# Two PSUM banks for transposes and one for weight products and first-chunk products, in place of one and two, in a windowed attention with two gated MLPs

## The chip, the cores and the metric

The kernel runs on one NeuronCore of a Trainium2 chip. The metric is the device time of one launch in microseconds (us); lower is better. The median of three runs before the change is 284.13 us (283.84 to 284.21). About 0.2% is what a measurement of this kernel can tell from no change.

## The reference

Attention over 2 batches, 8 heads, 768 positions and 64 values per head: each query sees the first 8 keys and the last 96. Its output feeds a gated MLP (a causal convolution of 5 taps makes the gate, one 512x512 product the value, a second the output), and that feeds another (512 to 1024, ReLU, a convolution of 3 taps as gate, 1024 to 512). Cut to what matters:

```python
scores = scale * np.matmul(q, k.transpose(0, 1, 3, 2)) + bias    # bias: -slope * distance
scores = np.where(keep, scores, -1000000000.0)                   # first n_global keys, last n_local keys
a = softmax(scores);  x = np.matmul(a, v)                        # x: (2, 768, 512)

gate = sigmoid(causal_conv5(x))                                  # first MLP
x = gate * (x @ w_val) @ w_out

h = np.maximum(x @ w_in, 0.0)                                    # second MLP
out = (h * sigmoid(conv3(h))) @ w_out2
```

## The kernel before

**Stages.** The attention goes through 12 tiles of 128 queries, 6 for each batch. For a tile, `scores` (L493, TensorE, marked `s` by the bank it writes) makes the scores of 4 heads at a time over its own and the tile of keys before it. `least` (L504, VectorE) adds the bias and takes the row minimum, `grow` (L509, ScalarE) the exponential and its sum, L530, L533 or L536 (VectorE, GpSimd or ScalarE) divide. `turn` (L563, TensorE, bank `t`) transposes the probabilities of two heads, 4 blocks of 128x128, into one bank; L567 (ScalarE) or L573 (VectorE) copies them out to `pts`; `output` (L588, bank `x`) multiplies by the values; L605 or L611 copies the result into `x`.

**Weights.** `product` (L337, bank `f`) multiplies the first MLP's output weight with the second's input weight, so that the two become one matrix W of 512x1024. It makes 8 products of 4 matmuls each; of each, `split_ops` writes a high part `Wh` (L244, ScalarE) and a low part `Wl` (L246, VectorE), and only the low part's end hands the bank on. `parts_unit` does the same for `w_val` (`wvh`, `wvl`), with no product.

**The MLPs.** The positions are cut into 4 chunks (2 for each batch, 400 and 368 columns). `values` multiplies a chunk by `w_val`: 4 products of 12 matmuls (L253 to L255, three for each block, of high and low parts), each taken out of its bank by the gate on VectorE (L759). `hidden` multiplies by W: 8 products of 12 matmuls, each taken out by a ReLU on ScalarE (L800). `project` writes the output in the four banks of the scores.

**Banks.** All 8 PSUM banks are in use: `BANKS` (L46) says 4 for `s`, 1 for `t`, 1 for `x` and 2 for `f`. `c.bank` gives the 12 products of the first chunk the ring `f`; later chunks, which start when the attention ends, take `f`, `t`, `f`, `x` in turn. A ring hands out its buffers one after the other, and a buffer's first instruction waits for the last user of the tenant before.

**Order.** A planner (`Plan`) sets the order of every engine's instructions. It knows an estimated cost for each step, the wait for a bank or buffer among its predecessors (`link`), and lays the steps in several passes by the length of what follows them (`lay`). Steps with several ways (dividing, the copies out of `t` and `x`, the masks, a convolution's first tap) go to the engine that ends them first. At run time each engine goes through its own list strictly in order.

Of the kernel before, what the change touches and what calls it, by code (L numbers as in the profile page):

```python
# [42 lines left out]
LANDED = {("k", 1): 3.0, ("k", 2): 5.0, ("r", 1): 6.3, ("v", 1): 7.7, ("r", 2): 9.0}  # L43
LANDING = 2.4
ORDERED = {getattr(mybir.EngineType, e) for e in ("PE", "DVE", "Activation", "Pool")}
BANKS = {"s": 4, "t": 1, "x": 1, "f": 2}  # L46


def slope(h):
# [819 lines left out]
def attention_gated_mlps(ctx, tc, kq, v, nn, w_val, conv_w, w_out, w_in2, w_out2, out):  # L869
# [50 lines left out]
    def arm(fast):  # L920
        with ExitStack() as es:
            psum = es.enter_context(tc.tile_pool(name="ps", bufs=1, space=PSUM))
            pools = es.enter_context(ExitStack())
            c.psum = Ctx()
            c.psum.tile = lambda shape, dt, tag, name: psum.tile(shape, dt, tag=tag, name=name, bufs=BANKS[tag])
            pl = c.plan = Plan()
# [15 lines left out]
            def bank(tag):  # L942
                return lambda: psum.tile([P, 512], F32, tag=tag, name=tag, bufs=BANKS[tag])

            def sb(pool, tag, shape, dt, n):
                return pl.ring(n, lambda: pool().tile(shape, dt, tag=tag, name=tag, bufs=n))

            c.ring = {t: pl.ring(n, bank(t)) for t, n in BANKS.items()}
            here = lambda: sg
# [97 lines left out]
```

## Time and profile before

| what | before |
|---|---|
| median of 3 runs | 284.13 us (283.84 to 284.21) |
| the profiled execution's own time | 283.84 us |
| its span, first to last instruction | 281.9 us |
| TensorE busy | 269.6 us (96%) |
| VectorE busy | 232.2 us (82%) |
| ScalarE busy | 194.8 us (69%) |
| GpSimd busy | 90.0 us (32%) |
| granted TensorE clock | 0.999 |

In the profile PE is TensorE, DVE VectorE, ACT ScalarE and POOL GpSimd. A matmul's duration includes its way through the array, and matmuls overlap, so a busy PE says little of how many it does; what one costs in a row of them is read from the starts of two neighbours in the timeline. One matmul of 32-bit floats in L337, L493 and L588 leaves two rows, so their counts in the trace are twice those in the program. A TensorE row that waited has the time and what ended it in brackets.

### The profile page before, as it was taken

What the parts mean: (1) busy time and instruction counts of PE and PEld (TensorE: products, weight loads), DVE (VectorE), ACT (ScalarE), POOL (GpSimd) and SP (SyncE); (2) the same over time, 40 slices, a digit from 0 to 9 for tenths busy, and PEclk for the clock granted to TensorE, in tenths of its full rate; (3) what the DMA queues carried; (4) which work ended last, traced back from release to release, by engine and by line L of the source; (5) the groups of instructions that cost most, each with busy time, mean ns of one, the idle gap of its engine ahead of it and who ended that gap; (6) DMA issues with size and microseconds to landing.
All of it is one profiled execution on the core that took longest, in us unless ns stands there. A gap on an engine that the chain in (4) does not pass through costs nothing.

```text
span 281.9 us, 5430 instructions
## 1 busy us (share of the span) xinstructions
PE 269.6 (96%) x1832; PEld 226.3 (80%) x1832; DVE 232.2 (82%) x587; ACT 194.8 (69%) x496; POOL 90.0 (32%) x199
## 2 busy tenths in 40 slices
PE   2889999999999999999999999999999999999993
PEld 2767675655458989999999999889999988899883
DVE  3989999999999999999999999999984654357600
ACT  2999989998678999886797456883473254544520
POOL 4635746346353336533256001140411000002000
PEclk9999999999999999999999999999999999999999
DMA  5983877446733431003300000100000020000121
GB/s 165 356 346 97 277 243 237 141 140 216 227 87 140 144 127 49 9 2 116 121 0 0 3 0 0 40 37 1 37 2 0 0 77 37 37 1 2 38 112 49
DMA packets 10420, 26.17 MB, mean 93 GB/s; under 512 B 1424, under 2 KB 2704, under 8 KB 10384
## 3 DMA queue, kind: packets, MB, share of 16 engines
q1 hardware_dynamic: 9968, 25.22, 26.4%
q10 hardware_dynamic: 416, 0.52, 0.5%
q8 instruction: 16, 0.26, 0.4%
q14 instruction: 20, 0.16, 0.2%
HBM read 22.59 MB, written 3.15 MB: 91 GB/s over the span
## 4 chain that ended last, share of the span: by engine, by line
PE 72%; DVE 21%; issue 3%; ACT 1%; DVEq 1%; POOL 0%
PE s L254 8%; PE s L255 8%; PE s L253 8%; PE f L253 7%; PE f L254 7%; PE f L255 7%; DVE p L504 5%; PE t L563 4%; PE x L588 4%; PE s L493 4%; DVE z L706 3%; DVE raw L279 3%; PE t L255 2%; PE x L255 2%; PE x L253 2%
## 5 line engine op out<-in xcount | busy, mean ns | idle before, releaser
L706 DVE SCALAR_TENSOR_TENSOR z<-h,cw,z 128x384 f32<-128x384 f32 x64 | 40.7, 642 | 12.8 <-ACT z L701 11.6
L509 ACT ACTIVATE p<-p,st 128x256 f32<-128x256 f32 (+1 forms) x96 | 46.0, 482 | 3.8 <-DVE st L504 2.9
L708 ACT ACTIVATE z<-z 128x384 f32<-128x384 f32 (+2 forms) x48 | 24.8, 523 | 26.3 <-DVE z L706 26.0
L706 DVE SCALAR_TENSOR_TENSOR z<-x,cw,z 128x400 f32<-128x400 f32 (+1 forms) x64 | 40.5, 666 | 0.1
L254 PE MATMUL s<-w,g 128*128 128x512 f32 (+1 forms) x104 | 39.2, 377 | 0.0
L255 PE MATMUL s<-w,g 128*128 128x512 f32 (+1 forms) x104 | 39.2, 377 | 0.0
L253 PE MATMUL s<-w,g 128*128 128x512 f32 (+1 forms) x104 | 39.1, 376 | 0.0
L337 PE MATMUL f<-w,w 128*128 128x512 f32 x64 | 31.9, 607 | 0.1
L563 PEld LDWEIGHTS t<-ident,p 128*128 128x128 f32 x176 | 20.0, 141 | 14.0 <-issue 4.3
L504 DVE CUSTOM_DVE_ANT_0 p<-s,B 128x256 f32<-128x256 f32 x80 | 30.9, 412 | 0.3 <-PE s L493 0.3
L563 PE MATMUL t<-ident,p 128*128 128x128 f32 x176 | 28.6, 281 | 2.1 <-ACT pts L567 1.0
L533 POOL TENSOR_SCALAR p<-p,st 128x256 f32<-128x256 f32 (+1 forms) x38 | 24.8, 658 | 12.4 <-DVE st L523 11.4
L253 PE MATMUL f<-gg,Wh 128*128 128x400 f32 (+1 forms) x80 | 27.7, 347 | 0.0
L255 PE MATMUL f<-gg,Wl 128*128 128x400 f32 (+1 forms) x80 | 27.0, 338 | 0.0
L254 PE MATMUL f<-gg,Wh 128*128 128x400 f32 (+1 forms) x80 | 27.0, 338 | 0.0
L702 POOL TENSOR_SCALAR z<-h,cw 128x384 f32<-128x384 f32 x11 | 9.7, 883 | 51.6 <-DVE z L706 31.0
L274 POOL TENSOR_SCALAR raw<-raw 128x512 f32<-128x512 f32 x24 | 19.4, 810 | 16.8 <-ACT m L272 8.6
L255 PEld LDWEIGHTS s<-w,g 128*128 128x128 f32 x104 | 19.5, 188 | 3.9
L246 DVE TENSOR_TENSOR g<-z,g 128x384 fp32r<-128x384 f32 x32 | 17.7, 564 | 5.9 <-ACT g L244 5.9
L253 PEld LDWEIGHTS s<-w,g 128*128 128x128 f32 x104 | 19.5, 188 | 2.8
L254 PEld LDWEIGHTS s<-w,g 128*128 128x128 f32 x104 | 19.5, 188 | 2.8
L244 ACT ACTIVATE g<-z 128x384 fp32r<-128x384 f32 x32 | 16.3, 518 | 7.8 <-DVE z L819 4.7
(126 smaller groups left out, 662.2 us busy)
## 6 DMA issues: line engine op xcount, KB each, us to landing
raw<-in_moe_w_out_dram SPq DMA_DIRECT2D x12, 512.0 KB, 3.4
raw<-in_moe_w_in_dram SPq DMA_DIRECT2D x8, 512.0 KB, 4.9
k<-in_kq_dram SPq DMA_DIRECT2D x7, 512.0 KB, 4.5
v<-in_v_dram SPq DMA_DIRECT2D x11, 256.0 KB, 4.2
out_dram<-o SPq DMA_DIRECT2D x11, 256.0 KB, 2.0
raw<-in_moe_w_val_dram SPq DMA_DIRECT2D x4, 512.0 KB, 3.4
kq<-in_kq_dram SPq DMA_DIRECT2D x3, 512.0 KB, 4.6
v<-in_v_dram SPq DMA_DIRECT2D x8, 64.0 KB, 3.0
```

Source lines behind the costliest of these rows:

```text
L246: "DVE", dve_us(n), lambda: nc.vector.tensor_tensor(lo(), src(), hi().bitcast(F32), ALU.subtract),
L253: nc.tensor.matmul(out, lh, rh, start=first, stop=False)
L254: nc.tensor.matmul(out, lh, rl, start=False, stop=False)
L255: nc.tensor.matmul(out, ll, rh, start=False, stop=last)
L274: "POOL", pool_us(n), lambda: nc.gpsimd.tensor_scalar(whole(), whole(), 0.0, 1.0, ALU.mult, ALU.mult),
L337: nc.tensor.matmul(ps.t, big["wot"].t.bitcast(F32)[:, e, cs], big[wi].t.bitcast(F32)[:, e, :], start=e == 0, stop=e == 3)
L504: nc.vector.tensor_tensor_reduce(w.t[:, :nk], sc, bias, -QKSCALE, 3.0e38, ALU.add, ALU.min, st.t[:, 0, h : h + 1])
L509: nc.scalar.activation(w.t[:, :nk], w.t[:, :nk], AF.Exp, bias=st.t[:, 0, h : h + 1], scale=-1.0, accum_out=st.t[:, 1, h : h + 1],)
L533: nc.gpsimd.tensor_scalar(w.t[:, :nk], w.t[:, :nk], st.t[:, 2, h : h + 1], 1.0, ALU.mult, ALU.mult)
L563: nc.tensor.transpose(o[:, z, n, :], p[2 * pr + z].t[:, n * P : (n + 1) * P], ident)
L706: nc.vector.scalar_tensor_tensor(z(), src(k), w()[:, k : k + 1], z(), ALU.mult, ALU.add)
L708: pl.add("ACT", act_us(n), lambda: nc.scalar.activation(z(), z(), AF.Tanh, scale=0.5), bufs, [], [token])
```

## The change

One line: the ring for transposes gets a second bank, and the ring of the weight products and the first chunk loses one.

```diff
-BANKS = {"s": 4, "t": 1, "x": 1, "f": 2}
+BANKS = {"s": 4, "t": 2, "x": 1, "f": 1}
```

`link` puts the new waits among the predecessors, and `lay` lays everything anew, so all engines have another order. The steps are the same ones, apart from those with several ways: VectorE loses 3 copies out of `x`, 2 of 512 and 1 of 256 columns out of `t`, ScalarE takes these up, and of the convolutions' first taps it takes 5 of 384 columns from GpSimd. The names of weight buffers differ by their number only (w_923 is w_924). The order of the loads on SyncE differs by neighbours that change places.

TensorE, tile 1 of the attention, behind its first scores: a piece of the difference (`t<-ident,p` are transposes, `x<-pts,x` is `output`).

```order
 L493 MATMUL s<-k_71 128x128 x2
-L563 MATMUL t<-ident,p 128x128 x4
-L588 MATMUL x<-pts,x 64x128 x4
-L563 MATMUL t<-ident,p 128x128 x2
+L563 MATMUL t<-ident,p 128x128 x8
 L493 MATMUL s<-k_71,k_72 128x128 x2
...
-L588 MATMUL x<-pts,x 64x128 x4
+L588 MATMUL x<-pts,x 64x128 x8
```

Transposes of four heads now stand in one row of eight, and the products with the values come behind the next scores.

TensorE, from the last weight product (`f<-w`) to the first value product (`f<-gx,wvh`), before:

```order
L337 MATMUL f<-w_923,w_521 128x512
L493 MATMUL s<-k_71,k_72 128x128 x2
...
L563 MATMUL t<-ident,p 128x128 x4
L493 MATMUL s<-k_72,kq 128x128 x2
...
L253 MATMUL f<-gx,wvh 128x400
L254 MATMUL f<-gx,wvh 128x400
```

and after:

```order
L563 MATMUL t<-ident,p 128x128 x8
L493 MATMUL s<-k_72,kq 128x128 x2
...
L337 MATMUL f<-w_924,w_522 128x512 x4
L563 MATMUL t<-ident,p 128x128 x4
L588 MATMUL x<-pts,v 64x128 x16
L253 MATMUL f<-gx,wvh 128x400
L254 MATMUL f<-gx,wvh 128x400
```

The last weight product is now one row of four, with four transposes and 16 `output` matmuls between it and the first value product, which takes the same bank. Ahead of the first value product stand 112 `output` matmuls, 120 transposes, 136 scores and 32 weight matmuls; before it was 96, 116, 136 and 32.

VectorE, around the last low part of W (`Wl<-f,Wh`), before:

```order
L246 TENSOR_TENSOR wvl<-m,wvh 128x512
L246 TENSOR_TENSOR gx<-x,gx 128x400
L706 SCALAR_TENSOR_TENSOR z<-x,cw,z 128x400
L246 TENSOR_TENSOR Wl<-f,Wh 128x512
L504 ISA p,st<-s,B 128x256
...
L759 SCALAR_TENSOR_TENSOR z<-z,f 128x400
```

and after:

```order
L246 TENSOR_TENSOR wvl<-m,wvh 128x512
L706 SCALAR_TENSOR_TENSOR z<-x,cw,z 128x400 x3
L504 ISA p,st<-s,B 128x256
...
L246 TENSOR_TENSOR Wl<-f,Wh 128x512
L573 COPY pts<-t 128x512
...
L759 SCALAR_TENSOR_TENSOR z<-z,f 128x400
```

Six score rows that stood behind the last `Wl` now stand ahead of it. Counted from the start, VectorE has 58 score rows of 256 columns ahead of that `Wl` (52 before), no copy out of `x` (2 before), 2 copies of 256 columns out of `t` (3 before), and as many of the rest within one each.

## Rows read from the trace of the kernel before

**Rows 1.** The page: busy us, share of the span and instructions of each engine.

```profile
PE 269.6 (96%) x1832; PEld 226.3 (80%) x1832; DVE 232.2 (82%) x587; ACT 194.8 (69%) x496; POOL 90.0 (32%) x199
```

**Rows 2.** The chain that ended last, in order of time: start us, us, what.

```profile
17.66 0.66 PE t L563 x4
...
37.10 0.41 DVE p L504
...
71.34 0.60 DVE x L611
...
98.81 0.44 PE t L563 x4
...
277.33 0.42 DVE o L858
```

**Rows 3.** Busy time by stretch: PE, PEld, DVE, ACT, POOL; clock, DMA share, GB/s.

```profile
10.00:20.00 10.00, 8.17 (x88) 5.84 (x88) 8.98 (x43) 10.00 (x35) 5.07 (x15) 1.00 1.03 390
20.00:30.00 10.00, 10.00 (x112) 7.68 (x114) 9.55 (x34) 9.98 (x32) 6.20 (x12) 1.00 0.40 126
30.00:40.00 10.00, 10.00 (x84) 6.57 (x83) 9.46 (x35) 8.54 (x30) 6.41 (x12) 1.00 0.77 251
...
210.00:220.00 10.00, 10.00 (x54) 9.28 (x53) 5.63 (x11) 4.32 (x9) 1.53 (x13) 1.00 0.00 0
```

**Rows 4.** TensorE's timeline, first tiles: start us, us, operation, [idle before <-releaser].

```profile
11.11 0.44 PE L563 MATMUL t<-ident,p 128*128 128x128 f32 x2 [0.62 <-ACT pts L567]
...
17.66 0.66 PE L563 MATMUL t<-ident,p 128*128 128x128 f32 x4 [0.95 <-DVE pts L573]
```

**Rows 5.** TensorE's timeline, weight products and value products of the first chunk.

```profile
63.73 4.46 PE L337 MATMUL f<-w,w 128*128 128x512 f32 x10
68.12 0.49 PE L493 MATMUL s<-k,k 64*128 64x128 f32 x4
...
86.16 0.43 PE L253 MATMUL f<-gx,wvh 128*128 128x400 f32 x1
...
88.73 1.97 PE L588 MATMUL x<-pts,v 128*64 128x128 f32 x32
90.63 0.45 PE L253 MATMUL f<-gx,wvh 128*128 128x400 f32 x1
...
92.90 0.60 PE L563 MATMUL t<-ident,p 128*128 128x128 f32 x4
93.25 0.43 PE L253 MATMUL f<-gx,wvh 128*128 128x400 f32 x1
...
98.65 0.60 PE L563 MATMUL t<-ident,p 128*128 128x128 f32 x4
99.17 0.49 PE L493 MATMUL s<-k,kq 64*128 64x128 f32 x4
...
100.27 1.09 PE L588 MATMUL x<-pts,v 128*64 128x128 f32 x16
...
107.57 0.60 PE L563 MATMUL t<-ident,p 128*128 128x128 f32 x4
```

**Rows 6.** VectorE's timeline, the same stretch.

```profile
85.84 0.68 DVE L246 TENSOR_TENSOR wvl<-m,wvh 128x512 fp32r<-128x512 f32 x1
...
87.87 0.68 DVE L246 TENSOR_TENSOR Wl<-f,Wh 128x512 fp32r<-128x512 f32 x1
88.47 0.41 DVE L504 CUSTOM_DVE_ANT_0 p<-s,B 128x256 f32<-128x256 f32 x1
...
90.53 0.56 DVE L759 SCALAR_TENSOR_TENSOR z<-z,f 128x400 f32<-128x400 f32 x1
```

**Rows 7.** ScalarE's timeline, a high part of W and the first ReLU.

```profile
83.78 0.58 ACT L244 ACTIVATE Wh<-f 128x512 fp32r<-128x512 f32 x1
...
109.80 0.49 ACT L800 ACTIVATE h<-f 128x400 f32<-128x400 f32 x1
```

## The prediction

> **What bounds the kernel now.** I read the busy times first, then the chain that ended last, then the busy time by stretch, then the timelines of the three engines around one place. TensorE is busy 96% of the span and VectorE 82% [rows 1]; both are shares over stages with different limits. The chain tells the stages apart [rows 2]: from 17.66 to 37.10 us it lies on TensorE, from there to 98.81 mostly on VectorE, and from 98.81 on TensorE alone until the last copy out starts at 277.33. The stretches say the same [rows 3]: VectorE idles 1.02, 0.45 and 0.54 us in the three tens from 10 to 40, so 2.0 us in all, and behind 210 it is half idle while TensorE never is. The granted clock is 1.00 in every stretch shown, the level of 2.4 GHz.
>
> In the middle stretch TensorE has little to give either. A weight matmul costs (68.12 - 63.73) / 5 = 0.88 us from start to start [rows 5], the eight products so 32 x 0.88 = 28 us, and transposes, scores and weight products follow each other there almost without a gap. So two engines are nearly full from 18 us on, and behind the attention only TensorE counts. The work on TensorE is the same after the change. The time is then decided by one question: how much TensorE work is done when the first value product of the first chunk starts (86.16 us before, [rows 5]), since from there on TensorE was never short of work.
>
> **The change part by part.** The sum goes from that place.
>
> Step 1, the start of the first value product. Before, there were two `f` banks, and the product could start with the bank of the last weight product but one; it ran while VectorE still had the last `Wl` to do (87.87, [rows 6]). Now there is one bank, so it must wait for the last `Wl`. That `Wl` ended at 88.47, where the next row starts. After the change VectorE has six more score rows ahead of it, which cost 90.53 - 88.47 = 2.06 us [rows 6], two copies out of `x` fewer at 0.60 [rows 2], and one copy of 256 columns out of `t` fewer, which I put at the price of a score row of the same width, 2.06 / 6 = 0.34. That is 2.06 - 1.20 - 0.34 = +0.5, and the rows that differ by one each leave about 0.1: the last `Wl` ends at 89.1, and the product starts at 89.2.
>
> Step 2, what TensorE has done by then. By the order it has 16 `output` matmuls and 4 transposes more behind it. The 16 (32 rows in the trace) cost 90.63 - 88.73 = 1.90, the 4 transposes 93.25 - 92.90 = 0.35 [rows 5]. Before, the same amount of work was done at 86.16 + 2.25 = 88.4. The lag is 89.2 - 88.4 = **+0.8 us**, and every matmul of the remaining 188 us stands behind it.
>
> Step 3, what the second transpose bank gives. Before, TensorE waited for the one bank twice at the start, 0.62 and 0.95 us [rows 4]; with rows of eight transposes these waits go, and two shorter ones. TensorE is on the chain there, but at step 1 VectorE is the late one, so the gain counts only as far as VectorE gets its scores earlier. VectorE's idle time from 10 to 40 us is 2.0 [rows 3], so the gain is between 0 and 2.0. I take the middle of the two waits' prices less a little, **-0.7 us**: the first wait lies where VectorE has masks to make anyway.
>
> Step 4, what the lost bank costs before step 1. Seven weight products now wait for the `Wl` of the one before. From one `Wl` to the next takes at least 4 x 0.88 + 0.58 for `Wh` [rows 7] + 0.60 for `Wl` = 4.7 us. VectorE's own list between the last two is 5 convolution taps and one `wvl` at some 0.60 each (88.47 - 87.87 is a row of that kind), six score rows of 2.06 and the `Wl`, 6.3 us; so the bank comes back in time with 1.6 us in hand, if ScalarE does its `Wh` at once. If not, transposes and scores stand behind the waiting matmul on TensorE, and VectorE's score rows wait for those. Bounds: 0, and VectorE idling from 44 to 89 us as it did from 10 to 40, where TensorE held it up: 2.0 / 30 x 45 = 3.0. I take **+0.4**, close to the near end because VectorE has work in hand between.
>
> Step 5, what the lost bank costs behind step 1. The second to fourth value product wait for the gate (L759) on the one before. By the order, two copies out of `t`, two score rows and two divisions stand between the last `Wl` and the first gate, some 2.5 us, so the gate ends near 92.2; the product runs from 89.2 to 91.5 (92.90 - 90.63 = 2.27 each, [rows 5]), and TensorE then has transposes and scores of 0.52 and 1.1 us (98.65, 99.17, 100.27) up to 93.1. No wait. The same for seven of the hidden products, which wait for a ReLU on ScalarE: the first ended at 107.57 [rows 5] and its ReLU at 110.29 [rows 7], 2.7 us later, where the new order has only 1.6 us of other work. As late as that each time would be 1.1 us a boundary; but then nothing asked for the bank. Later chunks take `f` every second product, with 2 us of another product between. Bounds: 0 and 3 boundaries at 1.1, so 3.3. I take **+0.3**, near the first gate's price.
>
> The copies that ScalarE takes over are hidden by its idle time (it works 8.54 of the 10 us behind 30, [rows 3]); they cost something only through step 4. The five taps that go from GpSimd to ScalarE belong to the second MLP, behind the first ReLU at 109.80 [rows 7], where TensorE alone counts. The loads that changed places with a neighbour cost nothing: the DMA share is 0.40 and 0.77 in the tens behind 20 [rows 3].
>
> The sum: 0.8 - 0.7 + 0.4 + 0.3 = +0.8 us. On the profiled execution's 283.84 us that is 284.6; that execution stands 0.29 under the median of 284.13, so the prediction is 284.9 us, with the span at 282.7.
>
> **A rule weighed.** The clock in [rows 3] is 1.00 also in the stretch where TensorE was busy for only 8.17 of 10 us. The Trainium skill, page "TensorE: Matmul & The Clock Gate", section "A second HAM failure mode: psum-queue depth-cycling", says that a kernel which cycles through its PSUM banks can leave small gaps often enough for the clock to swing between its levels. The rows do not bear that out here, since the waits of [rows 4] left the clock alone; were it to fall for one value product, that would cost about another 2.27 us [rows 5].
>
> **The rivals.**
>
> Faster: the waits of [rows 4] are worth their whole price. TensorE is on the chain from 17.66 to 37.10, so all 2.0 us of VectorE's idle time go, the last `Wl` comes at 87.1, and steps 4 and 5 cost nothing: 0.8 - 2.0 = -1.2, 282.9 us. For it: both engines wait there. Against it: some of the idle time is a startup that waits for loads.
>
> The same: both banks end as no difference. The evacuations are planned for, the banks come back in time, and the second transpose bank gives back what step 1 takes: 0.8 - 0.8 = 0, 284.1 us. The mechanism is that TensorE always found other work while it waited for a bank; from 98.81 on the chain shows no bank wait at all [rows 2]. The same page, section "HAM oscillation — how this bites in real kernels", tells of a kernel in which PSUM double-buffering gave no further gain; by that rule neither bank matters, which is this case.
>
> Slower by more: ScalarE is the late one. It has more of the copies, and it hands back the one `f` bank at the ReLUs and with `Wh` ahead of `Wl`. From the point where a ReLU or `Wh` comes more than 1.6 us after its product, TensorE stands with scores queued behind it, and VectorE with it. With 3.3 us of step 5, and step 3 eaten by step 4, the sum is 0.8 + 3.3 = +4.1, or 288.2 us. For it: the 2.7 us of the first ReLU. Against it: the planner knows these waits.
>
> The change does nothing of what it says: excluded by the order, which has the rows of eight.
>
> **How the numbers follow.** The forecast (lag of under 2 us, 283.6 to 286.1) has a chance of 0.46; of that, 0.13 lies within 0.2% of 284.13 (283.56 to 284.70) and 0.33 above. Faster has 0.27, the same by no bank mattering 0.14, ScalarE late 0.11, a fallen clock 0.02. So faster 0.27, the same 0.13 + 0.14 = 0.27, slower 0.33 + 0.11 + 0.02 = 0.46; 0.2% is about what a measurement can tell from no change. The range takes in the faster case with half a microsecond under it and most of the slower one: 282.4 to 287.6.
>
> **What would show it.** Step 1: the first value product starts right behind the last `Wl`, near 89, with TensorE's wait put down to VectorE's L246. Step 2: from there to the last matmul 188 us. Step 3: no brackets at the transposes before 18 us, and less VectorE idle time from 10 to 40. Step 4: brackets at L337 naming L246. Step 5: brackets at the first of 12 matmuls naming L759 or L800. I am wrong if the first value product starts before 88, if TensorE loses more than 3 us between it and the end, or if the chain behind 100 us lies on another engine.

## The result, and the profile after

The change costs time. The changed kernel takes 287.51 us (median of 18 runs, 286.04 to 288.69), the kernel before 284.12 in the same comparison; the ratio is 1.0104 with a 95% interval of 1.0086 to 1.0122. That is slower by 3.4 us, where +0.8 was forecast: the side was right, the time lies 0.1 under the upper end of the range, and the size was off by 2.6 us. The profiled execution took 288.69 us, the longest of the 18, so its trace shows more loss than the median has.

The page of after, to be laid beside [rows 1]: busy time, the clock in 40 slices, and the chain by engine.

```profile
PE 272.2 (95%) x1832; PEld 230.3 (80%) x1832; DVE 231.7 (81%) x582; ACT 199.9 (70%) x508; POOL 83.1 (29%) x192
...
PEclk9979999999999999999999999999999999999998
...
PE 51%; DVE 38%; issue 5%; ACT 2%; POOL 1%; POOLq 1%; DVEq 0%
```

The chain by engine on the page of before:

```profile
PE 72%; DVE 21%; issue 3%; ACT 1%; DVEq 1%; POOL 0%
```

No engine became the bound by its work: VectorE has half a microsecond less. But the clock has a dent in its third slice, and 38% of the chain lies on VectorE, where it was 21%.

After by stretch, the stretches of [rows 3], then the dent (PE, PEld, DVE, ACT, POOL busy; clock, DMA share, GB/s).

```profile
10.00:20.00 10.00, 8.56 (x80) 7.19 (x80) 7.94 (x38) 8.29 (x30) 4.77 (x14) 0.83 1.02 375
20.00:30.00 10.00, 9.96 (x120) 8.00 (x118) 9.79 (x34) 9.78 (x33) 5.78 (x13) 1.00 0.39 142
30.00:40.00 10.00, 9.60 (x106) 7.05 (x102) 9.64 (x40) 9.93 (x29) 5.94 (x12) 1.00 0.69 203
...
210.00:220.00 10.00, 10.00 (x53) 9.11 (x51) 6.18 (x12) 3.91 (x8) 0.64 (x4) 1.00 0.01 2
...
12.00:14.00 2.00, 0.71 (x4) 0.40 (x4) 2.00 (x10) 2.00 (x8) 1.46 (x4) 1.00 1.06 412
14.00:16.00 2.00, 2.00 (x23) 1.97 (x24) 1.90 (x8) 1.88 (x9) 0.00 (x0) 0.66 1.01 388
16.00:18.00 2.00, 2.00 (x22) 1.78 (x20) 1.28 (x8) 1.74 (x7) 0.60 (x2) 0.50 1.11 416
```

From 12 to 14 us TensorE works only 0.71 us; then its clock falls to 0.50, the level of 1.2 GHz. VectorE idles 2.06 + 0.21 + 0.36 = 2.6 us from 10 to 40, against 2.0 before. From 210 to 220 TensorE is as full as it was.

TensorE's timeline after: the first transposes (compare [rows 4]), three weight products, the first value product, and the two products that waited later on.

```profile
11.19 0.66 PE L563 MATMUL t<-ident,p 128*128 128x128 f32 x4
13.02 0.41 PE L563 MATMUL t<-ident,p 128*128 128x128 f32 x2 [1.17 <-DVE pts L573]
13.70 0.41 PE L563 MATMUL t<-ident,p 128*128 128x128 f32 x2 [0.27 <-DVE pts L573]
...
51.47 3.70 PE L337 MATMUL f<-w,w 128*128 128x512 f32 x8 [0.28 <-DVE Wl L246]
...
57.83 1.55 PE L337 MATMUL f<-w,w 128*128 128x512 f32 x3 [0.25 <-DVE Wl L246]
...
78.65 3.70 PE L337 MATMUL f<-w,w 128*128 128x512 f32 x8 [0.69 <-DVE Wl L246]
...
89.41 1.97 PE L588 MATMUL x<-pts,v 128*64 128x128 f32 x32 [0.28 <-ACT x L605]
91.44 0.45 PE L253 MATMUL f<-gx,wvh 128*128 128x400 f32 x1
...
147.34 0.44 PE L253 MATMUL f<-gx,wvh 128*128 128x368 f32 x1 [0.39 <-DVE z L759]
...
169.11 0.45 PE L253 MATMUL f<-gx,wvh 128*128 128x400 f32 x1 [0.51 <-ACT h L800]
```

The first value product comes at 91.44. By the prices of step 2 the same work was done at 86.16 + 2.25 = 88.41 before, so TensorE is 3.0 us late there by that estimate; the sum of matmuls used further down puts it at 2.4 to 2.8. Its last matmul starts at 281.91 (276.96 before), 4.95 late: 1.9 us more, or 2.1 to 2.5 by that sum, are lost behind the first value product.

### The profile page after: what moved, and what is told of

Same layout as the page of the kernel before. It is cut to its first block, busy times and chain, and to the rows that moved or that the text cites. A ratio compares the mean times of both kernels' runs of the same rounds, so it can differ in the third digit from the quotient of the medians.

```text
span 286.9 us, 5422 instructions
## 1 busy us (share of the span) xinstructions
PE 272.2 (95%) x1832; PEld 230.3 (80%) x1832; DVE 231.7 (81%) x582; ACT 199.9 (70%) x508; POOL 83.1 (29%) x192
## 4 chain that ended last, share of the span: by engine, by line
PE 51%; DVE 38%; issue 5%; ACT 2%; POOL 1%; POOLq 1%; DVEq 0%
DVE z L706 11%; PE s L255 7%; PE s L254 7%; PE s L253 7%; DVE p L504 6%; PE s L493 5%; DVE raw L279 4%; PE f L253 3%; PE f L255 3%; PE f L254 3%; PE x L588 3%; PE t L563 3%; DVE m L282 3%; DVE p L530 2%; PE x L255 2%
## 5 line engine op out<-in xcount | busy, mean ns | idle before, releaser
L706 DVE SCALAR_TENSOR_TENSOR z<-h,cw,z 128x384 f32<-128x384 f32 x64 | 39.4, 621 | 13.7 <-ACT z L701 12.2
L706 DVE SCALAR_TENSOR_TENSOR z<-x,cw,z 128x400 f32<-128x400 f32 (+1 forms) x64 | 41.2, 670 | 0.2
L337 PE MATMUL f<-w,w 128*128 128x512 f32 x64 | 30.4, 610 | 1.3 <-DVE Wl L246 1.2
L563 PE MATMUL t<-ident,p 128*128 128x128 f32 x176 | 25.4, 277 | 2.0 <-DVE pts L573 1.4
L533 POOL TENSOR_SCALAR p<-p,st 128x256 f32<-128x256 f32 (+1 forms) x35 | 21.0, 606 | 16.0 <-DVE st L523 15.0
L246 DVE TENSOR_TENSOR g<-z,g 128x384 fp32r<-128x384 f32 x32 | 17.8, 563 | 8.0 <-ACT g L244 8.0
L567 ACT ACTIVATE pts<-t 128x512 f32<-128x512 f32 (+1 forms) x38 | 20.8, 552 | 2.0 <-PE t L563 1.9
L819 DVE SCALAR_TENSOR_TENSOR z<-z,h 128x384 f32<-128x384 f32 x32 | 18.1, 569 | 4.9 <-ACT z L708 4.3
```

Source lines behind the costliest of these rows:

```text
L337: nc.tensor.matmul(ps.t, big["wot"].t.bitcast(F32)[:, e, cs], big[wi].t.bitcast(F32)[:, e, :], start=e == 0, stop=e == 3)
L533: nc.gpsimd.tensor_scalar(w.t[:, :nk], w.t[:, :nk], st.t[:, 2, h : h + 1], 1.0, ALU.mult, ALU.mult)
L563: nc.tensor.transpose(o[:, z, n, :], p[2 * pr + z].t[:, n * P : (n + 1) * P], ident)
L567: nc.scalar.activation(w.t[:, :, :nw, :], o[:, :, :nw, :], AF.Copy)
L706: nc.vector.scalar_tensor_tensor(z(), src(k), w()[:, k : k + 1], z(), ALU.mult, ALU.add)
```

## The experiments

Two theories stood against each other. **A**: the lost `f` bank holds TensorE up. **B**: any change of the banks makes the planner lay everything anew, each laying draws another order of all five engines with other small stalls, and the kernel before has a good one.

**Laying anew without changing a bank.** Two numbers of the planner's estimates were moved a little, for the old banks and for the new. Nothing else changes: same steps, same work; only the order differs, and which engine takes a step that several can.

```diff
-    LAG = {"PE": 0.2, "ACT": 0.15, "DVE": 0.15, "POOL": 0.15, "SP": 0.0, "AHEAD": 0.0}
+    LAG = {"PE": 0.22, "ACT": 0.15, "DVE": 0.15, "POOL": 0.15, "SP": 0.0, "AHEAD": 0.0}
```

The first pair, with the old banks (relay_before):

> The kernel before with its own banks; only the planner's allowance for a signal from TensorE goes from 0.20 to 0.22 us, so that everything is laid anew. Theory A (the lost f bank makes the loss: its waits hold TensorE up): banks as before, so 284.1, within 0.5 either way. Theory B (the order that a laying happens to give decides, and any new laying moves the time by up to about 1%): anywhere from 282 to 287.5, with a change of over 0.6 more likely than not.

and with the new (relay_after):

> The changed banks (t 2, f 1), with the same step of the planner's allowance from 0.20 to 0.22 us. Theory A: as the changed kernel, 287.5, within 0.7. Theory B: anywhere from 283 to 289, and if under 285 the lost bank is not the cause.

Measured: 287.34 us with the old banks (ratio 1.0129, 1.0078 to 1.0180), 286.65 with the new (1.0062, 1.0040 to 1.0084). The old banks, laid anew, lost about as much as the change did. Three more pairs followed, with `SWITCH` 0.12 in place of 0.10 (relay2), TensorE's `LAG` 0.18 (relay3) and `SWITCH` 0.08 (relay4):

```diff
-    SWITCH = 0.1
+    SWITCH = 0.12
```

> The kernel before, its banks untouched (one t, two f); only the planner's cost of a change between tiles is 0.12 in place of 0.10, so that the list is laid anew. Theory A (the lost f bank holds TensorE up): the old banks give the old time, 283.5 to 285.0, whatever the list. Theory B (each laying draws another order, and the kernel before had a lucky one): 285.5 to 288.5, as the first laying anew of the old banks gave 287.3.

> The changed kernel (two t, one f) with the same 0.12 in place of 0.10. Theory A: 286.5 to 288.5, the time of the change stays with its banks, and lies 2 us or more over the old banks laid with the same numbers. Theory B: anywhere from 284.5 to 288.5, and under the old banks about as often as over them.

> The kernel before, its banks untouched; the planner's lag of TensorE is 0.18 in place of 0.20. Theory A: 283.5 to 285.0. Theory B: 285.5 to 288.5.

> The changed kernel (two t, one f) with the planner's lag of TensorE at 0.18 in place of 0.20. Theory A: 286.5 to 288.5 and 2 us or more over the old banks laid with 0.18. Theory B: anywhere from 284.5 to 288.5, within 1.5 us of the old banks laid with 0.18 on either side.

> The kernel before, its banks untouched; the planner's cost of a change between tiles is 0.08 in place of 0.10. By theory B, which three layings anew of the old banks (287.3, 288.2, 290.0) have borne out: 286 to 290. Theory A would still have 283.5 to 285.0.

> The changed kernel (two t, one f) with the cost of a change at 0.08. By theory B 286 to 290, and within 2 us of the old banks laid with 0.08 on either side. If the banks have a worth of their own, as theory A has it, 2 us or more over the old banks laid with 0.08.

Measured, each against the kernel before:

| laid with | old banks | new banks | new less old |
|---|---|---|---|
| as given | 284.1, 1 | 287.5, 1.0104 | +3.4 us |
| TensorE's lag 0.22 | 287.3, 1.0129 | 286.7, 1.0062 | -0.7 |
| switch 0.12 | 290.0, 1.0193 | 289.5, 1.0174 | -0.6 |
| TensorE's lag 0.18 | 288.2, 1.0120 | 289.9, 1.0159 | +1.7 |
| switch 0.08 | 286.5, 1.0073 | 287.9, 1.0127 | +1.5 |

Over the four pairs that were laid anew the mean ratio is 1.0129 with the old banks and 1.0131 with the new. Each of the four old-bank layings is slower than the kernel before by 0.7 to 1.9%, and the changed kernel's 1.0104 lies under the mean of both columns. Theory A has the old banks keep the old time, and that was wrong four times; nor did the new banks lie 2 us over the old ones in any of these pairs. Theory B's ranges were too narrow in three runs: relay2's two kernels came out above its 288.5, and so did relay3_after, which also lies 1.7 us over its partner where 1.5 was allowed. The pairs differ by -0.7 to +1.7 us, so four of them leave room for a worth of the banks of a microsecond or two on either side, the forecast's +0.8 among it; what they show is that a new order alone costs as much as the whole change did. Whether the kernel before is good by chance or because its two numbers were chosen with these banks, these runs don't tell.

**One bank each, and the eighth bank given to one side or the other at a fixed order.** First the list was laid and run with one `t` and one `f` (t1_f1). Then that same list was run with the free bank given to `t`, and with it given to `f`; a list laid for fewer banks can be run with more. The difference against the changed kernel, for the bank given to `f`; given to `t`, `BANKS` stays and only `LAID` is new.

```diff
-BANKS = {"s": 4, "t": 2, "x": 1, "f": 1}
+BANKS = {"s": 4, "t": 1, "x": 1, "f": 2}
+LAID = {"s": 4, "t": 1, "x": 1, "f": 1}
...
-            c.ring = {t: pl.ring(n, bank(t)) for t, n in BANKS.items()}
+            c.ring = {t: pl.ring(n, bank(t)) for t, n in LAID.items()}
```

> One bank for transposes and one f bank, 7 banks in all, laid for that. Theory A: it has the lost f bank's cost and no second t bank, so at least the changed kernel's 287.5, and up to 289.5 by the transposes' waits of some 2 us at the start. Theory B: 283 to 290, with no order between it and the changed kernel.

> Every engine's order is that of the kernel with one t and one f bank, but two t banks are there at run time. It measures what the second t bank is worth with the order held fixed. Theory A and B alike: between 0 and 2 us less than that kernel; 0 to 0.3 if the order already has other work where the one bank makes TensorE wait.

> The list laid for one t bank and one f bank (292.7 when run with those), run unchanged with the eighth bank given to f: the same order as the run that gave it to t (292.6), so the two differ in the place of that bank and in nothing else. Theory A (the one f bank holds TensorE up): 289 to 291, since the weight products and the first value products no longer wait for an eviction. Theory B (the order decides, the place of the bank does not): 292.0 to 293.2, level with the other two.

Measured: 292.72 us with one each (1.0295, 1.0254 to 1.0337), 292.59 with a second `t` (1.0303, 1.0239 to 1.0368), 294.43 with a second `f` (1.0357, 1.0339 to 1.0376). The list laid for one bank each is slower than both theories had it, and with the second `f` it missed both again: A had a gain, B no difference. With the order held, neither bank shortens the launch. The waits for `Wl` at L337 were 0.7 us with one bank each, 1.5 with the second `t`, and are gone with the second `f`. By the sum of matmuls described below, TensorE with the second `f` is 1.4 us ahead of one bank each at 101 us and 2.2 ahead at 140, 0.5 of that from the start, before any `f` product. The lead then goes into a longer wait at 149 us, where a value product of the second chunk takes the `x` bank, and into the clock behind it. With the second `f` bank, TensorE's timeline (line numbers one higher) and the stretch after the wait (columns as above):

```profile
149.40 0.46 PE L254 MATMUL x<-gx,wvh 128*128 128x368 f32 x1 [2.42 <-ACT x L606]
```

```profile
150.00:152.00 2.00, 2.00 (x8) 2.00 (x7) 2.00 (x5) 2.00 (x6) 0.02 (x1) 0.50 0.00 0
```

That wait was 1.5 us with one bank each and 1.3 with the second `t` bank, and the clock stayed at 1.00 behind it in both. So theory A's time fails here too, for a list that was laid with one `f` bank in mind, though its mechanism shows: the second `f` bank does free TensorE by a microsecond or two, and the rest of the order takes it back. How the order of the changed kernel itself would run with a second `f` bank wasn't tried: all eight banks are taken.

**Taking the first value product out from under the one bank.** The weight products and the first chunk's products take `f` and the two `t` banks in turn.

```diff
-            ps = c.ring["f"].new()
+            ps = c.ring["ft"[cb % 2]].new()
...
-            c.bank = lambda b, ch: c.ring["f" if (b, ch) == chunks[0] else next(turn)].new()
+            first = iter("ft" * 6)
+            c.bank = lambda b, ch: c.ring[next(first) if (b, ch) == chunks[0] else next(turn)].new()
```

> The changed kernel, but the weight products and the first chunk's products take the f bank and the two t banks in turn, in place of f alone, and the list is laid with that. Theory A: 283.5 to 285.5, for the first value product no longer waits for the last copy of a weight and comes before 90 us. Theory B: it is one more laying anew, 286 to 290, even if the first value product comes early.

Measured: 295.63 us (1.0413, 1.0377 to 1.0448), the slowest of all, slower than theory B had it too. The first value product did come early, in a `t` bank at 81.80 us. The time went elsewhere. TensorE's timeline at 123 us, GpSimd's row that it waited for, and the stretches around it:

```profile
81.80 0.45 PE L253 MATMUL t<-gx,wvh 128*128 128x400 f32 x1
...
123.16 0.88 PE L563 MATMUL t<-ident,p 128*128 128x128 f32 x6 [2.43 <-POOL p L533]
```

```profile
120.96 3.25 POOL L533 TENSOR_SCALAR p<-p,st 128x256 f32<-128x256 f32 x4 [1.17 <-DVE st L523]
```

```profile
120.00:123.00 3.00, 0.63 (x4) 0.42 (x4) 3.00 (x8) 3.00 (x10) 2.04 (x3) 1.00 0.06 22
123.00:125.00 2.00, 1.61 (x9) 1.38 (x10) 2.00 (x5) 1.69 (x5) 1.86 (x5) 0.82 0.00 0
125.00:128.00 3.00, 3.00 (x11) 2.97 (x11) 3.00 (x7) 2.38 (x5) 2.52 (x4) 0.55 0.02 5
```

TensorE waited for divisions that stood in a row of four on GpSimd, and behind the gap its clock was 0.55. Around that place it lost 6.2 us to the kernel before, more than the whole change.

**Where each laying loses.** For every kernel I added up the matmuls in TensorE's timeline, each at its price in a row of its like (score 0.065, transpose 0.11, output 0.064, weight product 0.445, projection 0.2335, other products 0.182 us; score, weight and output rows at half a matmul each), and read when the same sum is reached as in the kernel before. The lag in us, from the profiled execution of each:

| kernel | at 18 us | at 101 | from 101 to the end | at the end |
|---|---|---|---|---|
| after | +1.5 | +2.6 | +2.4 | +5.0 |
| relay_before | +0.7 | +3.3 | -0.2 | +3.1 |
| relay2_before | -0.3 | +2.5 | +2.9 | +5.4 |
| relay3_before | +1.3 | +3.7 | +0.2 | +3.9 |
| relay4_before | +1.6 | +3.8 | 0.0 | +3.8 |
| relay_after | +1.1 | +2.2 | +1.0 | +3.2 |
| relay2_after | -0.3 | +2.9 | +1.7 | +4.6 |
| relay3_after | +2.7 | +2.5 | +3.8 | +6.3 |
| relay4_after | -0.9 | +1.0 | +2.1 | +3.1 |
| t1_f1 | +1.3 | +5.1 | +4.1 | +9.2 |
| alternate_f_t | -0.4 | +4.9 | +6.5 | +11.4 |

Hardly anything is lost behind 184 us in any of them. Among the four layings of each kind, the old banks lose 3.3 us on the mean up to 101 and 0.7 behind, the new ones 2.2 and 2.2. That fits a second `t` bank that helps in the attention and a lost `f` bank that costs in the chunks, at about the same price. Behind 98 us TensorE waits for a ReLU to hand back `f` in relay2_after, relay3_after and relay4_after, and in none of the old-bank layings. TensorE's waits behind 98 us, relay3_after (waited for: us in total, times, longest):

```profile
PE f L253 <- ACT h L800: 2.4, 3, 1.2
```

and relay2_before, the one old-bank laying that lost time there, its three longest:

```profile
PE t L563 <- POOL hb L805: 0.7, 1, 0.7
PE s L253 <- ACT g L244: 0.7, 1, 0.7
PE s L255 <- DVE g L246: 0.4, 1, 0.4
```

Four layings of a kind, which spread by 3 us behind 101, are too few to call the two shares shown, and the lags of after, relay_after, relay3_before and relay3_after hold a fall of the clock before 20 us besides. None of these kernels is as fast as the kernel before.

## Why the prediction was right, and where its size was wrong

**The place.** The first value product does start right behind the last `Wl`. VectorE's timeline after, its last `Wl`:

```profile
90.70 0.68 DVE L246 TENSOR_TENSOR Wl<-f,Wh 128x512 fp32r<-128x512 f32 x1
91.31 0.68 DVE L573 COPY pts<-t 128x512 f32<-128x512 f32 x1
```

The next row starts at 91.31, the product 0.13 later. But the bracket naming L246 that was announced isn't there: the 32 rows of `output` of 89.41 run up to 91.4. The product starts 0.34 us after the last of them started, where 0.20 is usual after such a row, so the wait for `Wl` held TensorE up by 0.14 us at most. That the two meet doesn't make the wait the cause of the lag: by the sum of matmuls TensorE was 1.5 us late at 18 us already and 2.7 at 84.

**Steps 1 and 2** put it at 89.2, a lag of +0.8; it is 91.44, a lag of 3.0, where steps 1 to 4 together had 0.5. The last `Wl` starts 90.70 - 87.87 = 2.83 us later than before [rows 6]. From 5 us to that row VectorE was busy 79.56 us before and 81.13 after, so its work there grew by 1.6, where +0.5 was counted from the rows that changed places; the rest is the balance of rows that were thought equal (four `gx` took 2.8 us in place of 2.3, four `wvl` 3.2 in place of 2.7, twelve `w` 8.4 in place of 9.1). And it idled 4.57 us in place of 3.31, which is 1.3 more. Of that, 1.2 lies before 20 us, where the clock fell. From 5 us to the last `Wl` and from 5 to 20 (columns as above), before:

```profile
5.00:87.87 82.87, 80.20 (x652) 52.67 (x653) 79.56 (x261) 74.34 (x223) 44.76 (x85) 1.00 0.65 218
5.00:20.00 15.00, 12.99 (x134) 10.27 (x136) 13.47 (x71) 14.68 (x54) 8.33 (x24) 1.00 0.97 349
```

and after:

```profile
5.00:90.70 85.70, 81.59 (x672) 56.72 (x674) 81.13 (x269) 76.86 (x232) 41.86 (x83) 0.98 0.65 211
5.00:20.00 15.00, 13.49 (x118) 11.82 (x120) 12.27 (x65) 12.95 (x48) 8.64 (x25) 0.89 0.96 340
```

**Step 3** failed. The second `t` bank was to give 0.7 us. The two waits of [rows 4], 0.62 and 0.95, are replaced by 1.17 and 0.27 at the first tile and a later one of 0.58 for a division: 2.0 us in all at the transposes, as before. The transposes of 13.02 wait for a copy out of `t`, and VectorE made that copy late. VectorE's timeline after:

```profile
11.56 0.42 DVE L504 CUSTOM_DVE_ANT_0 p<-s,B 128x256 f32<-128x256 f32 x1 [0.29 <-PE t L563]
...
11.91 0.42 DVE L504 CUSTOM_DVE_ANT_0 p<-s,B 128x256 f32<-128x256 f32 x1
...
12.25 0.29 DVE L530 TENSOR_SCALAR p<-p,st 128x128 f32<-128x128 f32 x1
12.46 0.41 DVE L573 COPY pts<-t 128x256 f32<-128x256 f32 x1
```

Two score rows and a division stand ahead of it. A bank comes free when the engine that empties it gets to it in its own list; the prediction took the second bank for the end of the wait and didn't look where the copy stands.

**Step 4** had the mechanism right and the size wrong: brackets at L337 naming L246 there are, three, 0.28 + 0.25 + 0.69 = 1.2 us, where 0.4 was taken. Before had none. They are not the one bank's alone, though: relay4_before, with its two `f` banks, has 1.0 us of them.

**Step 5** was to cost 0.3; behind the first value product 1.9 us were lost, or up to 2.5 by the sum of matmuls. Two brackets name the gate and a ReLU, 0.39 and 0.51, both in later chunks and not in the first one, where the step had looked. The chain after shows how the second comes about (start us, us, what):

```profile
168.06 0.63 ACT w L244
168.69 0.38 ACT h L800
169.07 0.04 issue
169.11 0.45 PE f L253
```

ScalarE did a part of a weight first, and the ReLU that hands the bank back came behind it. This is the "ScalarE late" rival, at one boundary and 0.5 us. It is also why the chain leaves TensorE: followed back from 169.11 it goes on over ScalarE and VectorE, so the last of the three signs that the prediction named against itself came true, though TensorE works 9.5 of 10 us there. By the sum of matmuls the lag is 2.8 us at 95 us, some 3.5 from 120 to 140, 4.2 behind the first of the two brackets and 4.9 behind the second, where it stays. So the two boundaries cost some 0.7 us each, a little more than their brackets say; the other 0.7, in the first chunk, has no bracket and stays open.

**The clock.** The rival of a fallen clock had a chance of 0.02 and +2.27 us. In the profiled execution it fell from 14 to 18 us. Over the 18 executions the granted clock says what that is worth: eight with 0.995 or more have a median of 286.5 us, six with 0.990 or less 288.4. So part of the median's +3.4 goes with a fall that happens in some executions, and some 2.4 us are there without one. The rule weighed there (the Trainium skill, page "TensorE: Matmul & The Clock Gate", section "A second HAM failure mode: psum-queue depth-cycling"), that small gaps from cycling through PSUM banks can swing the clock, was set aside by the rows of before. The trace of after agrees with it in part: a bank wait of 1.17 us stands before the fall, but the clock falls once and doesn't swing, and it fell in relay3_before too, with the old banks.

**What the prediction lacked** is the rival that the runs bear out: that the laying itself is a draw. It took before's order as what those banks give, and the new order as that order with a few rows moved. By the four old-bank layings, a new order costs some 3.7 us (1.3%) with the old banks, and by the other four about as much with the new; the forecast's sum of local terms came to +0.8 because each term was bounded by stalls that the old order had. The side came out right, and luck has a part in that: waits that the lost bank makes are in the trace (1.2 us at L337, 0.9 behind the first value product), but layings of the old banks with fewer such waits or none are as slow, and no run shows what the time would be without them.

## What to carry to other kernels

Where a planner lays a whole program, a one-line change of a resource is two changes: the resource, and a new order. Lay the old resources anew with a hair's change of the estimates, several times, before the difference is put down to the resource; here that spread was 0.7 to 1.9% against an effect of 1.0%. And a bank more doesn't end a wait for a bank unless the engine that empties it stands ready: look for the copy in that engine's list.

## What the runs showed of the hardware

I had not expected TensorE's clock to fall so near the start of a kernel that keeps it busy, nor that it differs between executions of one kernel. In four of the profiles of this study it stood at 0.50 from 14 to 16 or from 16 to 18 us: after, relay_after, relay3_before and relay3_after. Each time transposes had waited 1.3 to 2.1 us in all from 11 to 14 us, but the length of the wait alone doesn't tell: in relay_before they waited 0.66 and 0.90 there, in alternate_f_t 0.91 and 0.82, and the clock stayed at 1.00. The stretch from 14 to 16 us in relay3_before, columns as above:

```profile
14.00:16.00 2.00, 2.00 (x17) 1.78 (x18) 0.67 (x4) 1.34 (x6) 0.19 (x1) 0.50 1.02 395
```

At that level VectorE waits 1.33 us for scores and works 0.67 of the 2 us. The ten executions of relay_after fall into two groups by the clock: four at 0.997 or 0.998 took 285.4 to 285.6 us, six at 0.990 to 0.992 took 286.6 to 287.6. The profiled one, of the slower six, has its fall at the start; where the others have theirs isn't on record. If it is the same one, a fall at the start costs 1 to 2 us of the launch.
